# One pair of heads turned and hashed one slot sooner, and one sum of values moved ahead of the next pair, in a fused hash-attention and SwiGLU kernel

## The chip, the cores and the metric

The kernel runs on one core of a Trainium2 chip. The metric is the device time of one execution in microseconds (us); lower is better. The engines of the core run side by side, each through its own list of instructions in order, and wait for one another through semaphores: TensorE (PE: matmuls and transposes, into the accumulators of PSUM), VectorE (DVE), ScalarE (ACT), GpSimd (POOL) and SyncE (SP), which here issues DMAs.

## What is computed

For 4 batches of 8 heads with 768 positions of 64 values each, every query and key gets a bucket number from the signs of six random projections. Attention is limited to pairs of equal bucket. The result, as a matrix of 3072 rows by 512, goes through an RMS norm and a SwiGLU feed-forward layer of width 1536.

```python
q_bits = (einsum('bhsd,dk->bhsk', q, proj) > 0); k_bits = ...
mask   = bucket(q_bits)[:, :, :, None] == bucket(k_bits)[:, :, None, :]
scores = where(mask, q @ k.T / 8, -1e9)
attn   = exp(scores - max); attn = attn / (attn.sum(-1) + 1e-9)
x      = (attn @ v) laid out as (3072, 512)
xn     = x / sqrt(mean(x * x) + 1e-6) * rms_g
g      = xn @ w_gate
out    = (g * sigmoid(g) * (xn @ w_val)) @ w_out
```

## The kernel before, in words

**Slots.** The main loop runs over 192 slots (lines 876 to 881). A slot t issues, in this order: the scores of slot t + 1 (two matmuls of 128 by 384, line 345, into one of two score buffers `s_ps`), the exponentials of slot t on ScalarE (`probs`, line 357), and then whatever the list `plan[t]` holds. Three slots make one head of one half of a batch. The lists are written out by hand with `at(0, slot, function, ...)`: functions registered earlier in the code come first within a slot. In the first 37 slots there is no feed-forward work yet, and the feed-forward layer of the first half (u = 0) starts behind slot 37; from then on a planner (`spread`, line 792) fills the slots with gate, value and output matmuls by weights in ns.

**Preparing a pair of heads.** Heads are prepared in pairs (b, hp). For the pairs of batch 0 and the first two of batch 1, the work is:

- `load_natural` and `load_v` (lines 90, 104): three DMAs from SP.
- `turn_pe` (line 148), four times, in the order k of head 0, k of head 1, q of head 0, q of head 1: three transposes on TensorE into a PSUM bank `t_ps` (line 156), and one copy by VectorE into `kT` or `qT` (line 158).
- `cast_pool` (line 200): GpSimd casts `kT` or `qT` to half precision into the tile `QK`, rows 0 to 63.
- `hash_pair` (line 636): `hash_pairs` issues the projection's matmuls into two PSUM banks `d_ps` (line 236). The operands follow in the order k of head 0, q of head 0, k of head 1, q of head 1, so the last turn's copy is read by the fourth. Then VectorE makes sign bits from the two banks (`signs`, line 225).
- `send_pair` (line 640): four DMAs from SP carry the bits into rows 64 to 69 of `QK` (line 275).

All of this stands in one queue for each engine, in the order of the slots. PSUM banks named `t_ps`, `d_ps`, `m_ps` and later the feed-forward banks come in rotation from one pool of three (`bank`, line 84); a bank is used again when the engine that reads it is done.

**Values.** `av` (line 362) multiplies exponentials with values, nine matmuls of 65 columns in each of two slots of a head, into the single bank `o_ps`. `attn_out` (line 378) on VectorE adds the constant part `cvb` (`otmp`, line 384), takes the reciprocal, and multiplies, on GpSimd or, for the last pair of u = 0, on VectorE. `v_mean` (line 323) gives `cvb` for a pair from the sums of its values: for the pairs 1 to 3 of batch 0 six matmuls with ones into a bank `m_ps` (line 329), then one scaling by VectorE (line 332). The value matmuls of batch 0's heads 4 to 7 stand in slots 22 and 23, 25 and 26, 28 and 29, 30 and 31; `attn_out` in slots 26 (heads 4 and 5) and 31 (heads 6 and 7). Slot 31 is followed by the norm of u = 0 and, in slot 37, its turns `turn_x` (line 458).

**Around the change.** Before, in slots 21 to 32 and beside scores, exponentials and value matmuls, stand: in 21 `v_mean` of (0, 2); in 22 to 25 the four turns of pair (1, 0), with its cast of k in 24; in 26 its hash; in 27 the first turn of pair (1, 1); in 28 `v_mean` of (0, 3), the sends of pair (1, 0) and the second turn of (1, 1); in 29 and 30 the other two turns; in 32 the hash of (1, 1). Behind them come, on SP's queue, the block loads of pair (1, 2) in slot 34 (line 112), and on GpSimd's queue the loads of the feed-forward weights (`load_w`, line 580, in slots 22, 25 and 31, and later 39 and 42). Slots 34 to 36 hold a few matmuls without use (`z_ps`).

Of the kernel before, what the change touches and what calls it, by code (L numbers as in the profile page):

```python
# [33 lines left out]
def kernel(  # L34
# [559 lines left out]
    def at(w, s, f, *a):  # L594
        plan[NS * w + s].append(lambda: f(*a))
# [75 lines left out]
    at(0, 6, v_prep, 0, 1)  # L671
    at(0, 15, v_prep, 0, 2)
    at(0, 19, v_prep, 0, 3, nc.vector)
    for hp, t in enumerate((6, 16, 21, 28)):
        at(0, t, v_mean, 0, hp, 2, *([range(6)] if hp else []))
    for i, (t, t2) in enumerate(((22, 25), (31, 31))):
        cols = slice(i * DFF // 2, (i + 1) * DFF // 2)
# [2 lines left out]
        at(0, 39 + 3 * i, load_w, wo, moe_w_out, 6 * i, 6)  # L680


    for hp, ts in ((0, (8, 22, 23, 24, 25, 24, 39, 26, 28, 42)), (1, (20, 27, 28, 29, 30, 29, 41, 32, 33, 43))):
        tl, ts = ts[0], ts[1:]
        for w in "kq":
            at(0, tl, load_natural, nc.sync, 1, hp, w)
        at(0, tl, load_v, nc.sync, 1, hp)
        at(0, ts[0], new_pair, 1, hp)
        for t, hh, w in zip(ts[0:4], (0, 1, 0, 1), "kkqq"):
            at(0, t, turn_pe, 1, hp, hh, w)  # L690
        at(0, ts[4], cast_pool, 1, hp, "k")
        at(0, ts[5], cast_pool, 1, hp, "q")
        if hp == 0:
            at(0, ts[6], hash_pair, 1, hp)
            at(0, ts[7], send_pair, 1, hp)
        at(0, ts[8], v_prep, 1, hp)
        at(0, ts[8], v_sum, 1, hp)
# [33 lines left out]
    for n, (u, h) in enumerate(order):  # L731
        t = 3 * n + 4 - ((u, h) == (0, H - 1))
# [119 lines left out]
    def behind_norm(t):  # L852

        return t - t % NS + 9 if 1 <= t % NS < 9 else t

    for (b, hp), (load, kturns, qturns, _) in spots.items():
# [3 lines left out]
        for w, turns in (("k", kturns), ("q", qturns)):  # L860
            for i, t in enumerate(turns):
                at(0, t, turn_dve, b, hp, w, i, len(turns))
            t = turns[-1] + 1
            at(0, t if (b, hp) == (1, 2) else behind_norm(t), cast_pool, b, hp, w)
        t = 54 if (b, hp) == (1, 2) else behind_norm(qturns[-1] + 2)
# [69 lines left out]
```

## Time and profile before

| | us |
|---|---|
| median of 3 runs (lowest, highest) | 327.43 (327.17, 328.53) |
| the profiled execution | 327.66 |
| its span, first to last instruction | 325.9 |
| TensorE busy within the span | 321.1 |
| VectorE, ScalarE, GpSimd busy | 231.0, 228.6, 157.6 |

Times within the profile are in us from the span's start. The rows of a timeline give the start of the first of several equal instructions, the time from its start to the end of the last, the engine, the line of the kernel, the operation, what it writes and reads, its shape and how many there are; in brackets stands an idle time of over 0.15 us ahead of it and the instruction that ended it. Matmuls are pipelined, so records of TensorE overlap, and the time that one takes from the next is read from the distance of their starts.

Slots of the part in question, by the start of their scores on TensorE: slot 21 at 28.10, slot 22 at 28.89, slot 26 at 32.34, slot 27 at 33.93, slot 28 at 34.58, slot 32 at 38.33. The first gate matmul starts at 44.81.

### The profile page before, as it was taken

How to read it: one execution, taken by the hardware profiler on the slowest of the kernel's cores; microseconds unless marked ns; L12 is line 12 of the kernel's file. 1: busy time of each engine (PE TensorE's matmuls, PEld its weight loads, DVE VectorE, ACT ScalarE, POOL GpSimd, SP SyncE). 2: the span in 40 equal slices, each digit the busy share in tenths (PEclk: the TensorE clock that was granted, in tenths of full speed). 3: DMA queues.
4: the chain of work that ended last, by engine and by line, in shares of the span. 5: the costliest groups of instructions: out<-in, count | busy, mean ns of one | idle time of the engine just before them, and what ended most of it. 6: DMA issues, size and time to landing. Idle time of an engine off the chain costs nothing.

```text
span 325.9 us, 7789 instructions
## 1 busy us (share of the span) xinstructions
PE 321.1 (99%) x2954; PEld 194.6 (60%) x2955; DVE 231.0 (71%) x514; ACT 228.6 (70%) x333; POOL 157.6 (48%) x204
## 2 busy tenths in 40 slices
PE   9999999999999999999999999999999999999996
PEld 4576666656566565655566556655656556665554
DVE  5887876869878659875888558886677536673870
ACT  6999887666688667777767668776777768754322
POOL 3999749955974353732783522753592111221000
PEclk9999999999999999999999999999999999999999
DMA  7942999989328828253547047002200030003002
GB/s 227 348 159 65 229 216 208 178 120 183 115 41 157 158 61 170 49 105 99 82 107 145 7 139 138 7 1 58 80 4 3 1 99 32 2 2 101 14 2 97
DMA packets 85741, 32.63 MB, mean 100 GB/s; under 512 B 70908, under 2 KB 82632, under 8 KB 85704
## 3 DMA queue, kind: packets, MB, share of 16 engines
q1 hardware_dynamic: 81800, 27.35, 35.9%
q0 software_dynamic: 3680, 4.72, 8.7%
q8 instruction: 23, 0.38, 0.5%
q14 instruction: 14, 0.11, 0.1%
q10 hardware_dynamic: 224, 0.07, 0.1%
HBM read 28.58 MB, written 6.29 MB: 107 GB/s over the span
## 4 chain that ended last, share of the span: by engine, by line
PE 98%; ACT 1%; issue 0%
PE s_ps L345 20%; PE g_ps L480 19%; PE v_ps L480 19%; PE y_ps L509 18%; PE o_ps L370 11%; PE d_ps L216 2%; PE t_ps L156 2%; PE d_ps L236 2%; PE z_ps L576 1%; PE x_ps L463 1%; PE y_ps L528 1%; PE m_ps L329 1%; ACT psb L357 1%; PE s_ps L156 0%; ACT ypart L533 0%
## 5 line engine op out<-in xcount | busy, mean ns | idle before, releaser
L357 ACT ACTIVATE psb<-s_ps,ebias 128x768 f16<-128x768 f32 x192 | 167.9, 900 | 21.3 <-PE s_ps L345 20.4
L345 PE MATMUL s_ps<-QK 128*128 128x384 f16 (+1 forms) x384 | 93.5, 326 | 1.2 <-ACT psb L357 1.1
L488 ACT ACTIVATE t<-g_ps 128x384 f32<-128x384 f32 x96 | 47.2, 492 | 51.1 <-PE g_ps L480 49.4
L480 PE MATMUL g_ps<-xnT,wg 128*128 128x384 f16 x384 | 82.7, 326 | 0.0
L480 PE MATMUL v_ps<-xnT,wv 128*128 128x384 f16 x384 | 81.8, 326 | 0.0
L497 DVE SCALAR_TENSOR_TENSOR a<-t,g_ps 128x384 f32<-128x384 f32 x96 | 52.9, 551 | 27.1 <-ACT t L488 25.4
L391 POOL TENSOR_TENSOR x<-otmp,rcp 128x384 f32<-128x384 f32 x30 | 25.1, 838 | 97.1 <-DVE rcp L389 96.9
L509 PE MATMUL y_ps<-wo,ht 128*128 128x512 f16 x276 | 67.7, 379 | 0.0
L498 DVE SCALAR_TENSOR_TENSOR ht<-a,v_ps 128x384 f16<-128x384 f32 x96 | 53.2, 554 | 12.0 <-PE v_ps L480 4.1
L370 PEld LDWEIGHTS <-psb 128*128 128x128 f16 x1152 | 51.9, 97 | 15.7 <-issue 1.2
L370 PE MATMUL o_ps<-vl,psb 128*128 128x65 f16 x1152 | 55.8, 193 | 0.0
L345 PEld LDWEIGHTS <-QK 128*128 128x128 f16 (+1 forms) x384 | 34.7, 98 | 34.9 <-issue 9.2
L480 PEld LDWEIGHTS <-wg 128*128 128x128 f16 x384 | 35.2, 97 | 21.2
L480 PEld LDWEIGHTS <-wv 128*128 128x128 f16 x384 | 35.1, 97 | 20.8 <-issue 0.2
L509 PEld LDWEIGHTS <-ht 128*128 128x128 f16 x276 | 24.9, 98 | 23.0
L521 ACT COPY ysb<-y_ps 128x512 f32<-128x512 f32 x23 | 13.5, 587 | 16.0 <-PE y_ps L509 16.0
L384 DVE TENSOR_TENSOR otmp<-o_ps,cvb 128x390 f32<-128x390 f32 x32 | 17.8, 558 | 7.2 <-PE o_ps L370 7.2
L208 POOL CAST QK<-qT 64x768 f16<-64x768 f32 x20 | 16.5, 823 | 10.4 <-DVE qT L195 9.5
L397 POOL TENSOR_TENSOR sq<-x 128x384 f32<-128x384 f32 x24 | 19.9, 827 | 1.9
L208 POOL CAST QK<-kT 64x768 f16<-64x768 f32 x20 | 16.4, 822 | 4.7 <-DVE kT L195 2.7
L469 DVE TENSOR_TENSOR xnT<-x_ps,gcol 128x512 f16<-128x512 f16 x11 | 7.4, 688 | 15.0 <-PE x_ps L463 14.9
L195 DVE STREAM_TRANSPOSE kT<-kL 128x192 f32<-128x192 f32 x32 | 16.4, 518 | 0.0
(85 smaller groups left out, 277.3 us busy)
## 6 DMA issues: line engine op xcount, KB each, us to landing
vn<-in_v_dram SPq DMA_DIRECT2D x16, 384.0 KB
out_dram<-ysb SPq DMA_DIRECT2D x23, 256.0 KB
qL<-in_q_dram SPq DMA_DIRECT2D x40, 96.0 KB
kL<-in_k_dram SPq DMA_DIRECT2D x40, 96.0 KB
kn<-in_k_dram SPq DMA_DIRECT2D x5, 384.0 KB
qn<-in_q_dram SPq DMA_DIRECT2D x5, 384.0 KB
wg<-in_moe_w_gate_dram POOLq DMA_DIRECT2D x2, 768.0 KB, 9.9
wv<-in_moe_w_val_dram POOLq DMA_DIRECT2D x2, 768.0 KB, 12.1
```

Of the source, the lines that this page charges most:

```text
L208: nc.gpsimd.tensor_copy(QK[b, 2 * hp + hh, "h"][0:64, o : o + S], src[64 * hh : 64 * hh + 64, :])
L345: nc.tensor.matmul(ps[:, j, 0:HALF], QK[b, h, "h"][rows, S + jt * 128 : S + (jt + 1) * 128], QK[b, h, "h"][rows, half * HALF : (half + 1) ...
L357: nc.scalar.activation(psb[u, h][:, 2 * ch : 2 * ch + 2, :], sps.pop((u, i))[:, :, 0:HALF], AF.Exp, bias=ebias, scale=ESCALE,)
L370: nc.tensor.matmul(o[:, c, hh, 0:65], psb[u, h][:, jt, c * 128 : (c + 1) * 128], vls[b % 2][:, h, 2 * (jt % 3) + jt // 3 if b in PARITY el ...
L384: nc.vector.tensor_add(tmp[:, :, :, 0:65], o[:, :, :, 0:65], cvb[b % 2][:, 2 * hp : 2 * hp + 2, 0:65].unsqueeze(1).to_broadcast([128, 3, 2 ...
L391: eng.tensor_mul(xd.rearrange("p c (h d) -> p c h d", h=2), tmp[:, :, :, 0:64], r.to_broadcast([128, 3, 2, 64]),)
L397: eng.tensor_mul(sq, xd, xd)
L480: nc.tensor.matmul(ps, w[:, kt, fs], xnT[u][:, kt, :], start=(kt == 0), stop=(kt == 3))
L488: nc.scalar.activation(t, fbank[u, ft, "g_ps"], AF.Tanh, scale=0.5)
L497: nc.vector.scalar_tensor_tensor(out=a, in0=t, scalar=1.0, in1=g, op0=ALU.add, op1=ALU.mult)
L498: nc.vector.scalar_tensor_tensor(out=ht[u][:, ft, :], in0=a, scalar=0.5, in1=vv, op0=ALU.mult, op1=ALU.mult)
L509: nc.tensor.matmul(y, ht[u][:, ft, c * 128 : (c + 1) * 128], wo[:, ft, :], start=(ft == 0), stop=(ft == NF - 1),)
```

## The change

The four turns of pair (1, 0) move from slots 22, 23, 24, 25 to 21, 22, 23, 24. Its hash moves from slot 26 to 25 and the sends of its bits from slot 28 to 27. `v_mean` of pair (0, 3) moves from slot 28 to slot 26. The casts (k in slot 24, q in slot 39), the loads and the preparation of its values stay in their slots.

```diff
-    for hp, t in enumerate((6, 16, 21, 28)):
+    for hp, t in enumerate((6, 16, 21, 26)):
         at(0, t, v_mean, 0, hp, 2, *([range(6)] if hp else []))
...
-    for hp, ts in ((0, (8, 22, 23, 24, 25, 24, 39, 26, 28, 42)), (1, (20, 27, 28, 29, 30, 29, 41, 32, 33, 43))):
+    for hp, ts in ((0, (8, 21, 22, 23, 24, 24, 39, 25, 27, 42)), (1, (20, 27, 28, 29, 30, 29, 41, 32, 33, 43))):
         tl, ts = ts[0], ts[1:]
...
         at(0, ts[0], new_pair, 1, hp)
         for t, hh, w in zip(ts[0:4], (0, 1, 0, 1), "kkqq"):
             at(0, t, turn_pe, 1, hp, hh, w)
         at(0, ts[4], cast_pool, 1, hp, "k")
         at(0, ts[5], cast_pool, 1, hp, "q")
         if hp == 0:
             at(0, ts[6], hash_pair, 1, hp)
             at(0, ts[7], send_pair, 1, hp)
         at(0, ts[8], v_prep, 1, hp)
         at(0, ts[8], v_sum, 1, hp)
```

The tuple of a pair reads: slot of the loads; slots of the four turns; cast of k; cast of q; hash; sends; preparation of the values. Within a slot, `v_mean` is registered ahead of the pair's entries, and both ahead of the value matmuls. With the change the order on TensorE is: in slot 21 the sums of (0, 2) and then the first turn; in 22 and 23 a turn and the value matmuls; in 24 the last turn alone; in 25 the hash and the value matmuls; in 26 the sums of (0, 3) and the value matmuls; in 27 and 28 the first turns of pair (1, 1).

## The prediction

> **What bounds the kernel now.** I read the page first: which engine is full, and what carries the chain that ended last.
>
> ```profile
> PE 321.1 (99%) x2954; PEld 194.6 (60%) x2955; DVE 231.0 (71%) x514; ACT 228.6 (70%) x333; POOL 157.6 (48%) x204
> ...
> PEclk9999999999999999999999999999999999999999
> ...
> PE 98%; ACT 1%; issue 0%
> ```
>
> TensorE is busy for 321.1 of 325.9 us and carries 98% of the chain, at full granted clock. Since its records overlap, I don't take "busy" as proof; I compare starts. A pair of score matmuls advances the start of what follows by 0.33 us, three transposes by 0.33, nine value matmuls by 0.27 to 0.29, six of v_mean by 0.35. A larger step is a stall. By that count the stalls behind 45 us add up to about 2 us in all, so the end moves with the moment at which the first gate matmul starts (44.81 us), and the change acts ahead of it.
>
> Next I read the timeline of TensorE from slot 21 to slot 28; columns are start, length, engine, line, operation.
>
> ```profile
> 28.10 0.48 PE L345 MATMUL s_ps<-QK 70*128 70x384 f16 x2
> 28.43 0.51 PE L329 MATMUL m_ps<-vl,ones 128*128 128x130 f16 x6
> 28.89 0.48 PE L345 MATMUL s_ps<-QK 70*128 70x384 f16 x2
> 29.22 0.49 PE L156 MATMUL t_ps<-ident,kn 128*128 128x128 f32 x3
> ...
> 31.73 0.49 PE L156 MATMUL t_ps<-ident,qn 128*128 128x128 f32 x3
> 32.06 0.44 PE L370 MATMUL o_ps<-vl,psb 128*128 128x65 f16 x9
> 32.34 0.49 PE L345 MATMUL s_ps<-QK 70*128 70x384 f16 x2
> 32.76 0.51 PE L236 MATMUL d_ps<-kT,pj 64*32 64x384 f32 x2
> 32.77 0.51 PE L236 MATMUL d_ps<-qT,pj 64*32 64x384 f32 x2
> 32.78 0.51 PE L236 MATMUL d_ps<-kT,pj 64*32 64x384 f32 x2
> 32.87 0.51 PE L236 MATMUL d_ps<-qT,pj 64*32 64x384 f32 x2
> ...
> 33.64 0.45 PE L370 MATMUL o_ps<-vl,psb 128*128 128x65 f16 x9
> 33.93 0.49 PE L345 MATMUL s_ps<-QK 70*128 70x384 f16 x2
> ```
>
> Two things are to be seen. First, slot 21 (28.10 to 28.89) ends in a gap: v_mean's six matmuls are out at 28.43 + 0.35 = 28.78, and the next scores start at 28.89, because they need the score buffer of probs(21), whose exp runs from 27.94 to 28.85 in the trace. That is 0.12 us of stall. From there to the gate matmuls of slot 28 each step is of full size but one. Second, that one: within the hash, the fourth operand (q of the second head) starts at 32.87, 0.09 behind the third, where the others follow by 0.01. It waits for VectorE's copy of the last turn out of PSUM:
>
> ```profile
> 32.26 0.56 DVE L158 COPY qT<-t_ps 128x384 f32<-128x384 f32 x1
> 32.74 0.54 DVE L413 TENSOR_REDUCE ssp<-sq 128x3 f32<-128x384 f32 x1
> 33.75 1.02 DVE L225 TENSOR_SCALAR bits<-d_ps 128x384 uint16<-128x384 uint16 x2 [0.47 <-PE d_ps L236]
> 34.69 0.55 DVE L384 TENSOR_TENSOR otmp<-o_ps,cvb 128x390 f32<-128x390 f32 x1
> ```
>
> From the turn's first transpose to that hash matmul it takes 31.73 to 32.87, 1.14 us: 0.53 to the copy's start, 0.56 of copy, 0.055 to the matmul. The pairs of batch 0 show the same span where they wait: 12.86 to 14.00 and 18.52 to 19.66. The hash of pair (1, 1) doesn't wait: its operands start at 38.75, 38.76, 38.77 and 38.79, so 0.04 from first to fourth.
>
> **The change, part by part.** Nothing is added or removed. The number of transposes, hash matmuls, sums, copies and DMAs is as before; all that moves stays ahead of slot 31, whose value matmuls start the chain of copy, norm and turns that the gate matmuls wait for. So only stalls count.
>
> *The turns.* The first turn (0.33 us of TensorE) enters slot 21 behind v_mean, at 28.78, and fills the gap: the scores behind it start at 28.78 + 0.33 = 29.10 and their buffer is free since 28.85. Gain 0.12 us. Up to slot 24 TensorE is then 0.33 - 0.12 = 0.21 us later than before at equal slots, with one turn more behind it. The last turn, in slot 24, starts where the third did (behind scores(25) at 30.75) plus 0.21, thus at 30.75 + 0.21 + 0.33 = 31.29. The bank of each turn is the one used three banks before, which VectorE has emptied by 26.7 (the signs of pair (0, 3)), 29.3 or 29.9, all in time.
>
> *The hash, slot 25.* Before, nine value matmuls and one pair of scores stand between the last turn and the hash (slot 25 has value matmuls, slot 24 has none). After, slot 24 ends with the turn, so one pair of scores alone stands between. TensorE is free for the fourth operand at 0.33 (turn) + 0.42 (start of scores to start of hash, 32.34 to 32.76) + 0.04 = 0.79 us behind the turn's start; the operand is there at 1.14, since VectorE has nothing else to do just then (its reduction of slot 25 is queued behind the signs). The wait is 1.14 - 0.79 = 0.35 us, against 32.87 - 32.76 - 0.04 = 0.07 before (0.078 from unrounded starts). Loss 0.27 us. Queued behind it on TensorE are the value matmuls of slots 25 and 26 and scores(27) on; nobody else is late for it but ScalarE, whose next exp waits for those scores.
>
> *v_mean, 28 to 26.* Its 0.35 us are moved from between the second pair's first two turns to behind scores(27), with no step changed; what it reads (vl, cast by 27.2) is there. Its PSUM bank is that of the last q turn instead of a hash bank, free since about 32.4. On VectorE its scaling (0.28) now runs ahead of the value sums' copy (otmp) of slot 26 and no longer between the second pair's copies. Working VectorE's queue through from the signs (0.87 behind the fourth hash operand, at 31.29 + 1.14 = 32.43): signs 33.30 to 34.32, reduction from 34.24, scaling from 34.69, otmp from 34.89 to 35.45. The value matmuls of slot 28, which reuse otmp's bank, come at 35.74; slack 0.24. I cost this at nothing; if the cover went, the price is what exceeds 0.24.
>
> *Signs and sends.* The signs end at 34.32, not 34.77, so SP issues the four sends 0.45 us earlier, from about 34.35, with nothing before them in its queue (it is idle from 31.1 to 34.8). They end 0.45 us earlier, and so start the 8 loads of pair (1, 2) queued behind them (first at 37.74 before). POOL's casts keep their slots and are not the last to be ready; its first product of slot 26 comes 0.2 to 0.3 us later (behind otmp), which pushes the second half loads of the weights by as much; they land at 49.1 and 53.0 and are first read behind 55. The bits themselves are first read with the scores of batch 1, at 62.8: the earlier hash releases nobody early.
>
> **Sum.** -0.12 + 0.27 = +0.15 us at the first gate matmul (44.96), and at the end. The profiled execution took 327.66 (span 325.9), so it would take 327.81; it lies 0.23 above the median of 327.43, against which the forecast is 327.43 + 0.15 = **327.6 us**, no change that this measurement tells apart (about 0.5%, 1.6 us).
>
> **Rivals.** *The wait does not grow.* If the fourth operand had another reason to start at 32.87 than the copy, only the gap's 0.12 would remain: 327.3. Against it speak three equal spans of 1.14 us at different distances in the stream.
>
> *The banks bind.* If VectorE falls behind by more than the 0.24 of slack, the value matmuls of slot 28 wait for otmp. The queue holds 0.28 more ahead of otmp than before, so 0.1 to 0.3 us more: 327.9.
>
> *The weights come late (slower).* The loads of pair (1, 2) go out 0.45 us sooner and share the DMA engines with the first half of w_val, issued at 33.4 and landed 10.9 us later, at 44.35; the first value-feed matmul is at 45.46 and would be at 45.61. It decides from 1.26 us of delay on; each us beyond is a us at the end, so 0.5% needs a landing 2.9 us later, 47.3. Against it: 0.45 us of extra company can take at most 0.45 us from that load. At that point, 329.1.
>
> *The clock falls (slower).* In the first 4.6 us, z_ps matmuls follow each other at 0.43 us, later at 0.22 (the granted clock reads full in both, so spacing is the evidence); a second such stretch at half rate, at least 3.9 us long, would cost 1.9 us or more: 329.5. It would need a stall that the array's rate doesn't survive. The stalls of 0.92 at 9.0 and 0.55 at 26.7 are both longer than the new 0.35, and the scores behind the second follow at 0.16, full rate. The Trainium skill, "TensorE: Matmul & The Clock Gate", section "A second HAM failure mode: psum-queue depth-cycling", speaks for this rival: it reports that short idles between groups of matmuls, by cycling PSUM banks, made the clock gate swing. The same page's Part 1 lets the clock fall only after an idle window of about 3.4 us; by that, nothing happens here, and the trace's full rate behind 0.55 us agrees.
>
> *It does what it says, but something behind 45 us re-aligns.* About 2 us of stalls are left there; gaining 1.6 would need most of them to go. I see no mechanism.
>
> **Chances.** Forecast 0.70; wait does not grow 0.12; banks bind 0.11; weights 0.02; clock 0.02; re-alignment by over 0.5% faster 0.03. So same 0.93, slower 0.04, faster 0.03. Range: from 327.3 less the 0.26 by which the lowest run lies under the median, 327.0, to 327.9 plus about half of the 1.1 by which the highest lies over it, 328.5.
>
> **What would show it.** Right: scores(23) at 29.10; last turn at 31.29; fourth hash operand 1.14 us behind it and about 0.39 behind the first; value matmuls of slot 25 at 33.19; scores(28) at 34.42; the first gate matmul at 44.96. Wrong: a fourth operand that starts sooner than 1.1 us behind its turn; a gap ahead of the value matmuls at 35.74; a gap at the first value-feed matmul; stalls behind 45 us that differ by more than a few tenths.

## The result, and the profile after

| | before | after |
|---|---|---|
| median of 20 runs (lowest, highest) | 327.67 us (327.17, 328.53) | 328.22 us (327.62, 328.61) |
| ratio, 95% interval | | 1.0015 (1.0008 to 1.0022) |
| the profiled execution; its span | 327.66; 325.9 | 328.61; 326.5 |
| start of slot 20's scores | 27.31 | 27.87 |
| from there to the first gate matmul ("the stage") | 17.50 | 17.66 |
| from the first gate matmul to the end | 281.07 | 280.94 |
| time less span | 1.78 | 2.15 |

The medians differ by 0.55 us (0.17%), and the ratio of the runs is 1.0015: no change by the bound of 0.5%, but more than the 0.15 us of the forecast. The table splits the two profiled executions. The stage that the change touches is 0.16 us longer. But slot 20, ahead of which nothing changed, starts 0.56 later, and the time outside the span (ahead of the first recorded instruction and behind the last) is 0.37 longer. With the 0.13 less behind the first gate matmul, these add up, but for rounding, to the 0.95 us between the two executions. The ends of the stage, before and after:

```profile
27.31 0.48 PE L345 MATMUL s_ps<-QK 70*128 70x384 f16 x2 [0.39 <-ACT psb L357]
44.81 0.81 PE L480 MATMUL g_ps<-xnT,wg 128*128 128x384 f16 x4
```

```profile
27.87 0.48 PE L345 MATMUL s_ps<-QK 70*128 70x384 f16 x2 [0.39 <-ACT psb L357]
45.53 0.81 PE L480 MATMUL g_ps<-xnT,wg 128*128 128x384 f16 x4
```

The page after reads much as before:

```profile
PE 321.7 (99%) x2955; PEld 194.7 (60%) x2955; DVE 230.6 (71%) x514; ACT 228.7 (70%) x333; POOL 157.6 (48%) x204
...
PE 98%; ACT 1%; issue 0%
```

The timeline of TensorE after, for the slots that were shown of before (take 0.56 off each start to compare):

```profile
28.66 0.48 PE L345 MATMUL s_ps<-QK 70*128 70x384 f16 x2
28.98 0.51 PE L329 MATMUL m_ps<-vl,ones 128*128 128x130 f16 x6
29.33 0.49 PE L156 MATMUL t_ps<-ident,kn 128*128 128x128 f32 x3
29.66 0.49 PE L345 MATMUL s_ps<-QK 70*128 70x384 f16 x2
...
31.85 0.49 PE L156 MATMUL t_ps<-ident,qn 128*128 128x128 f32 x3
32.18 0.49 PE L345 MATMUL s_ps<-QK 70*128 70x384 f16 x2
32.60 0.51 PE L236 MATMUL d_ps<-kT,pj 64*32 64x384 f32 x2
...
32.99 0.83 PE L236 MATMUL d_ps<-qT,pj 64*32 64x384 f32 x4
33.76 0.45 PE L370 MATMUL o_ps<-vl,psb 128*128 128x65 f16 x9
```

The gap of slot 21 is gone: sums at 28.98, turn at 29.33, scores at 29.66, each a full step. The last turn starts at 31.85, the first hash operand at 32.60, and the fourth at 32.99, 1.14 behind the turn and 0.39 behind the first. VectorE's copy of that turn, and what follows on its queue:

```profile
32.38 0.56 DVE L158 COPY qT<-t_ps 128x384 f32<-128x384 f32 x1 [0.37 <-PE t_ps L156]
33.86 1.02 DVE L225 TENSOR_SCALAR bits<-d_ps 128x384 uint16<-128x384 uint16 x2 [0.92 <-PE d_ps L236]
34.80 0.54 DVE L413 TENSOR_REDUCE ssp<-sq 128x3 f32<-128x384 f32 x1
35.26 0.28 DVE L332 TENSOR_SCALAR cvb<-m_ps 128x130 f32<-128x130 f32 x1
35.46 0.55 DVE L384 TENSOR_TENSOR otmp<-o_ps,cvb 128x390 f32<-128x390 f32 x1
```

The copy ends at 32.94, 0.055 ahead of the operand that reads it.

So the theory is: TensorE's stalls are of two kinds, the copy's latency and the score buffers that ScalarE frees, and the change trades 0.12 us of the second for 0.27 of the first; the rest of the 0.55 does not come from stalls. Its rivals: the loss sits elsewhere in the stage; or the changed kernel starts later.

### The profile page after: what moved, and what is told of

Same layout as the page of the kernel before. It is cut to its first block, busy times and chain, and to the rows that moved or that the text cites. A ratio compares the mean times of both kernels' runs of the same rounds, so it can differ in the third digit from the quotient of the medians.

```text
span 326.5 us, 7788 instructions
## 1 busy us (share of the span) xinstructions
PE 321.7 (99%) x2955; PEld 194.7 (60%) x2955; DVE 230.6 (71%) x514; ACT 228.7 (70%) x333; POOL 157.6 (48%) x204
## 3 DMA queue, kind: packets, MB, share of 16 engines
q1 hardware_dynamic: 81800, 27.35, 36.1%
## 4 chain that ended last, share of the span: by engine, by line
PE 98%; ACT 1%; issue 0%
PE s_ps L345 20%; PE g_ps L480 19%; PE v_ps L480 19%; PE y_ps L509 18%; PE o_ps L370 11%; PE d_ps L216 2%; PE t_ps L156 2%; PE d_ps L236 2%; PE z_ps L576 1%; PE x_ps L463 1%; PE y_ps L528 1%; PE m_ps L329 1%; ACT psb L357 1%; PE s_ps L156 0%; ACT ypart L533 0%
## 5 line engine op out<-in xcount | busy, mean ns | idle before, releaser
L384 DVE TENSOR_TENSOR otmp<-o_ps,cvb 128x390 f32<-128x390 f32 x32 | 17.8, 556 | 7.2 <-PE o_ps L370 7.2
```

The lines of the kernel that those rows point to most:

```text
L384: nc.vector.tensor_add(tmp[:, :, :, 0:65], o[:, :, :, 0:65], cvb[b % 2][:, 2 * hp : 2 * hp + 2, 0:65].unsqueeze(1).to_broadcast([128, 3, 2 ...
```

## The experiments

In each, the stage is measured as in the table. The span of an unprofiled execution is on record to 0.1 us, so its time outside the span is known to 0.05.

**The same two kernels again.**

> The kernel before, unchanged, once more. Measure used in all runs: the stage from the start of slot 20's scores on TensorE (27.31 us in the profile before) to the first gate matmul (44.81): 17.50 before, 17.66 after, so +0.16, the forecast's +0.15. But the profile after is 0.56 us later already at slot 20, where no instruction has changed, and the medians of 20 runs differ by 0.55. Theory A: the part ahead of slot 20 differs from execution to execution of one and the same kernel (the moment at which the first matmuls turn from half to full rate); then this run shows a stage of 17.50, a start of slot 20 anywhere from 27.2 to 27.9, and a ratio of 1.000 within 0.1%. Theory B: the start belongs to the kernel; then slot 20 starts at 27.3 here, within 0.05.

> The changed kernel, unchanged, once more. Theory A (the change costs 0.16 us in its stage and nothing elsewhere; the rest of the 0.55 is the spread of the start): stage 17.66, slot 20 anywhere from 27.2 to 27.9, ratio 1.0005 with an interval that holds it. Theory B (the changed kernel starts later by 0.5 us, by the layout of its instructions or otherwise): slot 20 at 27.87 within 0.05, ratio 1.0015 to 1.002.

Stages 17.50 and 17.66, as before to 0.002 us; slot 20 starts at 27.35 and 27.30. So the late start of the first profile after doesn't belong to the changed kernel. The ratios are 1.0011 (1.0000 to 1.0022) for the kernel before against itself, which shows how much such a ratio wanders, and 1.0026 (1.0012 to 1.0039) for the changed one, more than 0.16 us can make; between the medians of the two kernels run again it is 0.59 us (327.88 and 328.47). Theory A holds for the start, and B falls there; but A's 1.0005 falls too. What stands out is the time outside the span: 1.75 to 1.86 us in 34 executions of the kernel before that ran beside these, 2.10 to 2.19 in all 31 of the changed kernel.

**The wait covered.** In the changed kernel, the hash of slot 25 is registered behind the value matmuls:

```diff
-            at(0, ts[6], hash_pair, 1, hp)
...
         for part in range(2):
             at(0, t + part, av, u, h, part)
+        if t == 25:
+            at(0, 25, hash_pair, 1, 0)
```

> The changed kernel, with the hash of slot 25 issued behind that slot's nine value matmuls instead of ahead of them. Theory (the new wait for the last turn's copy, 0.35 us, is the whole loss; nine value matmuls cover 0.28 of it): the fourth hash operand still 1.14 us behind the last turn's first transpose, the stage 17.66 - 0.28 = 17.38, thus 0.12 below before, the gap of slot 21. Rival (the loss sits in the order of the hash and the sums or in VectorE's queue, not in the copy's latency): the stage stays at 17.6 or more. In time -0.12 us against before, too little to tell from 1.000 by runs.

```profile
30.86 0.49 PE L156 MATMUL t_ps<-ident,qn 128*128 128x128 f32 x3
31.18 0.49 PE L345 MATMUL s_ps<-QK 70*128 70x384 f16 x2
31.51 0.43 PE L370 MATMUL o_ps<-vl,psb 128*128 128x65 f16 x9
31.88 0.51 PE L236 MATMUL d_ps<-kT,pj 64*32 64x384 f32 x2
...
32.00 0.51 PE L236 MATMUL d_ps<-qT,pj 64*32 64x384 f32 x2
...
83.50 0.48 PE L345 MATMUL s_ps<-QK 128*128 128x384 f16 x2 [1.08 <-DMA QK<-bits]
```

The stage is 17.38, as expected: the operand still comes 1.14 behind the turn (30.86 to 32.00), and the value matmuls fill the time. The loss was the copy's latency. The median is 328.13, ratio 1.0017 (1.0005 to 1.0029), with 2.10 to 2.22 us outside the span. The time thus misses the expected -0.12: with 0.36 more outside the span it should be +0.24 us or 1.0007, which the interval holds. The last line is a stall that this one execution met far behind the change: the scores of pair (1, 2) waited 1.25 us (by starts) for their bits, sent behind SP's block loads.

**The wait made longer.** The changed kernel with the hash in slot 24 instead of 25 (`(8, 21, 22, 23, 24, 24, 39, 24, 27, 42)`).

> The changed kernel, with the hash in slot 24, right behind the last turn: the suspected wait made longer. Theory: the fourth operand still starts 1.14 us behind the turn's first transpose, so the wait grows from 0.35 to about 0.7, 0.33 us more, and scores(29) then waits another 0.1 for its buffer: stage 18.0 to 18.1. Rival (the loss does not come from the copy's latency): 17.66. Time outside the span: TensorE 5535, VectorE 500, so 2.15 by either.

```profile
31.29 0.49 PE L156 MATMUL t_ps<-ident,qn 128*128 128x128 f32 x3
31.71 0.51 PE L236 MATMUL d_ps<-kT,pj 64*32 64x384 f32 x2
...
32.43 0.84 PE L236 MATMUL d_ps<-qT,pj 64*32 64x384 f32 x4
33.20 0.50 PE L345 MATMUL s_ps<-QK 70*128 70x384 f16 x2
```

31.29 to 32.43: 1.14 again, and the stage is 18.04. Whatever stands between turn and hash, the operand is ready at the same distance; what TensorE lacks to fill it is the stall.

**One part of the change alone.** First the turns, hash and sends without the sums:

> Before, with the pair's turns, hash and sends one slot sooner, and the sums of (0, 3) left in slot 28. Stage = from slot 20's scores to the first gate matmul (17.50 before, 17.66 after). Theory (stalls of TensorE of two kinds, the copy's latency and the two score buffers): without the sums in slot 26 TensorE reaches scores(29) at about 34.73, while probs(27), which frees the buffer, ends at 34.96; a new stall of 0.28, stage 17.94. Rival (the move of the sums is inert): 17.66. Second question, the time outside the span, which has been 1.79 us for the kernel before and for spread and 2.15 for the changed kernel and av_first in every execution: if it goes by the number of TensorE's instructions (waits counted: 5534 before, 5532 spread, 5535 the changed kernel, av_first and this one) it is 2.15 here; if by VectorE's (501 before and here, 502 spread, 500 the changed kernel and av_first) it is 1.79.

```profile
34.77 0.49 PE L345 MATMUL s_ps<-QK 70*128 70x384 f16 x2
35.09 0.49 PE L156 MATMUL t_ps<-ident,kn 128*128 128x128 f32 x3
35.70 0.48 PE L345 MATMUL s_ps<-QK 70*128 70x384 f16 x2
```

From the turn at 35.09 to the scores at 35.70 it is 0.61 us where 0.33 is a full step: 0.28 of stall, released by the exp of slot 27, which ends at 35.65, and a stage of 17.94. The sums' move is thus not inert: in slot 26 they fill time in which TensorE would run into ScalarE. Outside the span: 1.78 us, though TensorE's number of instructions is that of the changed kernel; that guess falls, and VectorE's number stays.

Then the sums alone (`(6, 16, 21, 26)`), and the changed kernel with the sums in slot 25 (`(6, 16, 21, 25)`):

> Before, with the sums of (0, 3) alone moved from slot 28 to 26, where they stand ahead of the hash, which stays in slot 26. Theory: they cover what is left of the wait for the last turn's copy (0.08 us), so the fourth hash operand follows the third by 0.01 and the stage is 17.42. Rival (no wait on the copy): 17.50. Time outside the span: TensorE has 5533 instructions here and VectorE 500; 1.79 if TensorE's number decides, 2.15 if VectorE's does.

> The changed kernel, with the sums of (0, 3) in slot 25 ahead of the hash instead of in slot 26. Theory: the sums cover the whole wait of 0.35 us, but then slot 26 holds only scores and value matmuls, TensorE reaches scores(29) 0.28 us before ScalarE has freed its buffer, and only 0.07 of the 0.35 is kept: stage 17.59. Rival (the copy's latency is the only bound): 17.31. Time outside the span: TensorE 5534, VectorE 500; 1.79 if TensorE's number decides, 2.15 if VectorE's does.

```profile
30.19 0.48 PE L345 MATMUL s_ps<-QK 70*128 70x384 f16 x2 [0.16 <-DMA QK<-bits]
...
33.48 0.51 PE L236 MATMUL d_ps<-kT,pj 64*32 64x384 f32 x2
...
33.52 0.51 PE L236 MATMUL d_ps<-qT,pj 64*32 64x384 f32 x2
...
35.55 0.49 PE L156 MATMUL t_ps<-ident,kn 128*128 128x128 f32 x3
35.99 0.43 PE L370 MATMUL o_ps<-vl,psb 128*128 128x65 f16 x9
```

With the sums alone (the lines above) the hash operands follow each other by 0.01, so the 0.08 is gone as expected; but the stage is 17.84, not 17.42. The trace names both differences: 0.32 at slot 23's scores, which waited for the bits of pair (0, 3) from their DMA (the kernel before with one more memset, below, met 0.24 there; the kernel before met none in either of its profiles), and 0.10 at slot 28's value matmuls (35.55 to 35.99 where 0.33 is a full step), which waited for `otmp`. So this run is a miss as a measure of the time. The second term is a wait for `o_ps`, the bank that the "banks bind" rival names, but not by that rival's cause: `otmp` starts 1.90 us behind the first hash operand, against 1.93 in the kernel before, so VectorE isn't later. TensorE is sooner: the sums no longer stand between the hash and slot 28's value matmuls, which would follow the hash by 2.40 us instead of 2.83. Together 17.50 - 0.08 + 0.32 + 0.10 = 17.84.

```profile
34.61 0.49 PE L156 MATMUL t_ps<-ident,kn 128*128 128x128 f32 x3
35.22 0.49 PE L345 MATMUL s_ps<-QK 70*128 70x384 f16 x2
```

With the sums in slot 25 (these two lines) the stage is 17.62 for 17.59 expected: of the wait for the last turn's copy 0.04 is left, and slot 28's scores then wait 0.28 for their buffer. Both runs have 2.13 to 2.14 us outside the span, as VectorE's number has it.

**The time outside the span.** The trace of the kernel before holds 697 records of VectorE's queue, 180 of them waits; of the changed kernel, 696 and 179. The traces show where one goes: before, a record of its own, a wait for VectorE's own earlier work, stands ahead of `otmp` of slot 31 (L384, at 37.67); after, there is none, and `otmp` waits for TensorE alone. In the changed order the scaling already lies ahead of the `otmp` of slot 26. In the next two runs the number of VectorE's instructions is changed by one memset among the first instructions. The changed kernel gets one more:

```diff
     nc.vector.memset(mhalf, -0.5)
+    nc.vector.memset(cvb[1][0:32, 0, 64:66], 0.0)
```

In the kernel before, GpSimd takes one over:

```diff
-    nc.vector.memset(mhalf, -0.5)
+    nc.gpsimd.memset(mhalf, -0.5)
```

> The changed kernel with one more instruction on VectorE, a memset of 32 by 2 numbers among the first ones, so that its trace should hold 697 VectorE records (waits counted) again, as the kernel before, spread and turns_only do, and not 696, as the changed kernel and all others with its order of the sums do. Theory (the 0.36 us outside the span goes by the number of VectorE's instructions, not by the order of the work): time less span 1.79 us, stage 17.66, ratio to before 1.0005 (0.16 of 327.65). Rival (it goes by where the sums stand): time less span 2.15, ratio 1.0015 to 1.002.

> The kernel before with one memset of VectorE (128 by 3 numbers, needed late) given to GpSimd, so 696 records on VectorE and 264 instead of 263 on GpSimd. Theory: time less span 2.15 us, stage 17.50, ratio 1.0011 (0.36 of 327.65). Rival (the number has no part in it): 1.79, ratio 1.000.

The changed kernel with one more: 697 records, 1.75 to 1.83 us outside the span in 11 executions, stage 17.66, ratio 1.0006 (0.9997 to 1.0015). The kernel before with one fewer: 696 records, 2.10 to 2.19 in 10 executions, stage 17.49, ratio 1.0011 (1.0001 to 1.0020). Both as the theory has it.

> The kernel before with one more memset on VectorE, 698 records. If the time outside the span is 2.15 for every number below 697 and 1.79 above: 1.79. If it alternates between odd and even numbers: 2.15.

> The kernel before with two memsets of VectorE given to GpSimd, 695 records. If the time outside the span is 2.15 for every number below 697: 2.15. If it alternates: 1.79.

With 698 records it is 1.87 us, with 695 2.11, one execution each. So between 695 and 698 it is a step, from 696 to 697, not an alternation. What happens in those 0.36 us lies outside the records, and stays open. The Trainium skill, "Runtime: NRT & Kernel Launch", section "Instruction fetch mechanics", says that each engine's instructions are fetched in blocks and that crossing a block is mostly hidden. Blocks could make a step. No run here shows that this is it, nor why the smaller number should be the slower: in the span the instruction queue q14 has 14 packets with 695, 696, 697 and 698 records alike, and q8 has 23.

**A version from the theory.** Against the kernel before:

```diff
-    for hp, t in enumerate((6, 16, 21, 28)):
+    for hp, t in enumerate((6, 16, 21, 24)):
...
-    for hp, ts in ((0, (8, 22, 23, 24, 25, 24, 39, 26, 28, 42)), (1, (20, 27, 28, 29, 30, 29, 41, 32, 33, 43))):
+    for hp, ts in ((0, (8, 19, 20, 22, 23, 24, 39, 25, 27, 42)), (1, (20, 26, 27, 28, 30, 29, 41, 32, 33, 43))):
```

(The expectation names the slots of the sums wrongly; the diff has them: those of pair 2 stay in 21, those of pair 3 go to 24.)

> A version that follows from the theory: turns of pair (1, 0) in slots 19, 20, 22, 23, its hash in 25, the sums of pair 2 and 3 in slots 24 and 26 (26: value sums' order kept for slot 24 and 28 as before), the turns of pair (1, 1) in 26, 27, 28 and 30. It fills the stalls ahead of slots 20 to 22 (0.55, 0.20 and 0.12 us before) and leaves 1.2 us between the last turn and the hash. Theory (only stalls of TensorE count, of two kinds: the copy's latency and the score buffers that ScalarE frees each 0.78 us): the stage 17.50 - 0.52 = 16.98 and 0.5 us less in time, ratio 0.9985. Rival (the stage is set by ScalarE's 0.78 us a slot and the chain behind slot 31): 17.3 to 17.5.

```profile
29.81 0.49 PE L156 MATMUL t_ps<-ident,qn 128*128 128x128 f32 x3
...
31.51 0.51 PE L236 MATMUL d_ps<-kT,pj 64*32 64x384 f32 x2
31.52 0.51 PE L236 MATMUL d_ps<-qT,pj 64*32 64x384 f32 x2
31.54 0.52 PE L236 MATMUL d_ps<-kT,pj 64*32 64x384 f32 x2
31.55 0.51 PE L236 MATMUL d_ps<-qT,pj 64*32 64x384 f32 x2
```

1.7 us lie between last turn and hash, and the four operands follow by 0.01. The stage is 17.06 (16.98 expected, 17.50 before), and the kernel is faster than both: 327.35 us, ratio 0.9986 (0.9978 to 0.9995) to the kernel before. It has 697 records on VectorE, and 1.73 to 1.84 us outside the span.

## Why the prediction was right, and where it was short

Counted from slot 21's scores, to take the start out:

- *The turns.* Scores(23) were to start 1.00 us behind and the last turn 3.19; they do (29.66 and 31.85 less 28.66). The gap's 0.12 was gained.
- *The hash.* Forecast: the fourth operand 1.14 behind its turn and 0.39 behind the first, value matmuls at 5.09. Measured 1.14, 0.39 and 5.10. The latency was read right, and the three other orders in which the operand is waited for (av_first, hash_24, turns_only) have the same 1.14 within 0.01. What follows keeps step: slot 27's scores, called scores(28) in the forecast, at 6.33 (6.32) and the first gate matmul at 16.87 (16.86).
- *The sums, signs and sends.* Signs at 5.20, `otmp` at 6.80 (6.79 forecast), sends at 6.25 as forecast; no gap ahead of the value matmuls of slot 28. The move was costed at nothing and cost nothing, but for a reason that the working didn't name: without it, the same change would have lost 0.28 more to the score buffers.
- *Behind the gate.* Nothing realigned: 280.94 against 281.07 us.
- *The rivals.* The wait grew; no bank bound, in the changed kernel; the first half of w_val was in time (no gap at the value matmuls of the first feed). The clock held: after the new wait of 0.35 us, the next two score matmuls start 0.17 us apart, full rate. The Trainium skill, "TensorE: Matmul & The Clock Gate", Part 1, lets the clock fall only after an idle window of about 3.4 us, and this trace agrees.
- *What was short.* The step "the profiled execution took 327.66 (span 325.9), so it would take 327.81" held the time outside the span at 1.78 us. It became 2.15. The sum of the two is 0.16 + 0.36 = 0.52, against 0.55 measured between the medians; the forecast's 0.15 had only the first. That the two agree to 0.03 is in part luck, since the kernel before, run against itself, moved by 0.23 (327.88 to 327.65). And the forecast of 327.6 stood on the median of three executions, 327.43, which is 0.24 under that of twenty: of the 0.64 us by which 328.22 lies above 327.58, 0.24 is that base and 0.36 the time outside the span.

That it came out as "no change" says little about the mechanism, for any change under 1.6 us would have done so. The rows of the stage are what bears it out.

The late start of the first profile after belongs to that execution and is no difference between the kernels: the changed kernel, run again, starts slot 20 at 27.30. Over the profiles, slot 20 starts between 26.88 and 27.99 us, and in the 12 of 14 that have a clock record it follows the moment at which that record begins with full rate: 3.83 and 26.88 (av_first), 4.76 and 27.30 (after_again), 6.53 and 27.87 (the first profile after), 6.78 and 27.99 (turns_only). The Trainium skill, "TensorE: Matmul & The Clock Gate", Part 1, says that the gate opens by a window that runs freely of the kernel's start, so that the moment differs from run to run; the traces agree that it differs. The same Part 1 of the Trainium skill puts that difference at plus or minus 500 ns; here there are 3 us between the earliest moment and the latest, and 1.1 us of it in the start of slot 20.

## What to carry to other kernels

Between a turn and what reads its copy lies a fixed latency (here 1.14 us from the first transpose); count the work that the queue holds in between, and move something there before moving the reader. In the same sum keep the other bound, the buffers that a second engine frees at its own rate: a slot too light loses as surely as one that waits. And split a difference of medians by stage, start, and time outside the span, for a part of it may come from no stall at all.

## What the runs showed of the hardware that was not expected

- One instruction fewer on VectorE (696 records for 697) made every execution about 0.36 us longer, outside the first and last recorded instruction: 1.73 to 1.86 us against 2.10 to 2.22. Taking one memset away or adding one brings it about; why stays open.
- The bits that SP sends are at times late. In one execution of av_first, sends behind SP's block loads cost 1.25 us of stall at 82 us. In one each of mean_only and before_dve_more, the sends of pair (0, 3), with no load ahead of them, cost 0.32 and 0.24 at slot 23; the other profiles show no wait for bits over 0.15. In those last two a packet of the instruction queue q14 falls among the sends (at 28.55 and 28.82 us), and in no other profile; no run shows whether it delays them. Late bits and the clock's start can make up part of the 1 to 2 us by which executions of one kernel differ.
